# Swapping W_in's halves on VectorE instead of TensorE, in a convolution + GELU feed-forward kernel

## The chip, the cores and the metric

One core of a Trainium2 chip runs the whole kernel. The time is device microseconds of that core, the median over several executions. An execution under the hardware profiler gives the trace; all instants below are microseconds from the start of the profiled span, and an instruction's time is what the trace gives for it.

The engines: TensorE (PE) multiplies, VectorE (DVE), ScalarE (ACT) and GpSimd (POOL) work on vectors, SyncE (SP) only issues transfers. SP, ACT and POOL each have a DMA queue: q1 is SP's, q10 ACT's and q0 POOL's. All three are served by the same 16 DMA engines.

## What is computed

Input x is 8 sequences of 4096 tokens with 192 channels. A causal convolution of 7 taps runs along each sequence; its weights are a softmax over the taps, one set for each of 8 heads of 24 channels. Then a two-layer network: 192 to 2048, exact GELU, 2048 to 192.

```python
w = np.exp(weight - max) ; w = w / (sum(w) + 1e-9)        # (8 heads, 7 taps)
x_pad = zeros(6 tokens) followed by x                      # in each sequence
conv[b, s, h, g] = sum_k w[h, k] * x_pad[b, s + k, h, g]
h = conv.reshape(32768, 192) @ w_in                        # 192 x 2048
out = (gelu(h)) @ w_out                                    # 2048 x 192
```

Everything goes in and out in float32; inside, the matrices and activations that PE reads are bf16.

## The kernel before

**Layout.** The 32768 tokens are split into two halves. Partitions 0 to 63 hold channels of the first half's tokens, partitions 64 to 127 the same channels of the second half's, so that PE does two products of 64 rows side by side. 192 channels are three groups `p` of 64. The tokens go by in blocks, per half: four blocks of 256 tokens, then blocks of 512 (`WS`, L33).

**Weights in SBUF.** W_in (`win`) is loaded once, half of its columns to each half of the partitions: partitions 0 to 63 get columns 0 to 1023, partitions 64 to 127 columns 1024 to 2047 (`win_in`, L227). Each half needs the other half's columns too, so what lies on one half is copied across to the other. Before, PE does that: `dup` (L537) multiplies with an identity (`idb`), placed so that the result comes out on the opposite partitions, in PSUM, and DVE evicts it to `win` (`dup_out`, L341), in four steps of 256 columns. POOL issues the load in two parts: columns 0 to 255 of each half, then the other 768; behind them W_out (`wout`, L268).

**A block's stages.** Loads of x go into one of three buffers `xin` (`load`, L169; four DMAs for each block). DVE transposes 32x32 squares to have channels on the partitions (`trans`, L363); POOL adds the halo of six earlier tokens (`halo`, L273). The convolution of blocks 3 and on is done by DVE as 21 multiply-adds per block (`conv`, L382). That of the first three blocks (`ND`) is done by PE (`pconv`, L559): for each tap a product with a diagonal matrix (`dg`, written by `diag`, L333) of the tap's weights; the result is in PSUM and is evicted as bf16 (`conv_out`, L356; for block 0 ACT, L488). For the products, block 0's transposed x is cast by ACT (L480), that of blocks 1 and 2 by DVE (`cast`, L349).

**The network.** A block has slices: 8 of two 128-column chunks of W_in for 256 tokens, 16 of one chunk for 512. `mm1` (L599) makes a slice in one of two PSUM buffers `hp`, ACT applies GELU from PSUM into `gT` (L509), and `mm2` (L626) multiplies `gT` with W_out. The second layer of block n - 1 is spread over the slices of block n; in block 1 it starts at slice 2 and first waits for W_out. A group `g` is 128 tokens of the second layer; its result is evicted by DVE (`evac`, L409) and stored by SP. Group 1 of block 0 and the products of block 2's convolution use the same PSUM buffer (`ob[1]`), so that group waits for all three evictions of block 2 (L636); the third product of block 2 waits for the eviction of the first (L573), with which it shares a bank.

**Order.** Each engine works through a list written by hand, in order. PE: 5 spins (products whose result nobody reads), the products that spread the tap weights, 8 spins, block 0's convolution with the first swap step inside, then the slices; the table `behind` (L594) says which swap step or convolution stands behind which slice: swap steps 1 to 3 behind slices 1 to 3 of block 0, block 1's three products behind slices 4 to 6, block 2's behind slices 1 to 3 of block 1. DVE: the softmax's small operations, `diag`, block 0's transposes, the swap evictions, blocks 1 and 2, then the convolutions of block 3 and on, with the evictions `evac` at the places that the table `late` gives as (block, operation). SP: x for block 0 and, when the first part of W_in has landed, for blocks 1, 2, 3; then one further load and one store for each block (L687 on). Of blocks 0 and 1, ACT issues half of the loads.

**Tap weights.** The softmax gives 8x7 numbers on 8 partitions. Each channel's partition needs those of its head: POOL makes a 0/1 matrix `sel` with two selects (L237, L247), PE multiplies (L529), and DVE copies the result to `wcol` (L329).

Of the kernel before, what the change touches and what calls it, by code (L numbers as in the profile page):

```python
# [5 lines left out]
ALU = mybir.AluOpType  # L6
AF = mybir.ActivationFunctionType
BF16 = mybir.dt.bfloat16
F32 = mybir.dt.float32


def bass_lightweight_conv__then__act_gelu_exact_kernel(
# [76 lines left out]
    with es:  # L89
# [7 lines left out]
        wnm = sbt("wnm", [H, KS], F32)  # L97
        sel = sbt("sel", [H, NP * 128], F32)
        wcol = sbt("wcol", [128, NP * KS], F32)
# [15 lines left out]
        S_WIN = [sem("S_WIN%d" % i) for i in range(2)]  # L115
# [4 lines left out]
        S_SEL = sem("S_SEL")  # L120
        S_IDN = sem("S_IDN")
        S_PEP = sem("S_PEP")
# [5 lines left out]
        S_CAST = sem("S_CAST")  # L128
        S_PC = sem("S_PC")
        S_PCE = sem("S_PCE")  # L130
        S_DUP = sem("S_DUP")
# [13 lines left out]
        DUPB = [hp[0], ob[1], ob[0], ob[1]]  # L145
# [8 lines left out]
        FH = F // 2  # L154

# [70 lines left out]
        def _(g):  # L226
            def win_in(c0, c1, sm):  # L227
# [5 lines left out]

            win_in(0, FQ, S_WIN[0])
            g.wait_ge(S_MSET, 2)
            pat = [[64, NP], [0, 2], [1, 64]]
            g.affine_select(  # L237
                out=sel[:, :],
                in_=sel[:, :],
                compare_op=ALU.is_ge,  # L240
                fill=0.0,
                base=0,
                pattern=pat,
                channel_multiplier=-GRP,
            ).then_inc(S_SEL)
            g.wait_ge(S_SEL, 1)
            g.affine_select(  # L247
                out=sel[:, :],
                in_=sel[:, :],
                compare_op=ALU.is_ge,  # L250
                fill=0.0,
                base=GRP - 1,
                pattern=[[-a, b] for a, b in pat],
                channel_multiplier=GRP,
            ).then_inc(S_SEL)
            for hf in range(2):
# [10 lines left out]
            win_in(FQ, FH, S_WIN[1])  # L267
            g.dma_start(  # L268
                ap(wout, 0, [[NF * C, 128], [C, NF], [1, C]]),
                ap(woutt, 0, [[C, 128], [128 * C, NF], [1, C]]),  # L270
            ).then_inc(S_WOUT, 16)
# [36 lines left out]
            for n in range(NB):  # L308
                halo(n)

        @block.vector
        def _(v):
            v.memset(warm[:, :], 0.0).then_inc(S_WARM)  # L313
            v.memset(sel[:, :], 1.0).then_inc(S_MSET)
            v.memset(idb[:, :], 1.0).then_inc(S_MSET)
            v.wait_ge(S_WSB, 16)
# [7 lines left out]
            v.wait_ge(S_PRO, 3)  # L324
            v.tensor_scalar(
# [7 lines left out]
            def diag(p):  # L333
# [4 lines left out]
                    ALU.mult,  # L338
                ).then_inc(S_DG)

            def dup_out(s):  # L341

                v.wait_ge(S_DUP, s + 1)
                v.tensor_copy(  # L344
# [386 lines left out]
```

## Time and profile before

| | us |
|---|---|
| median of 11 runs (lowest to highest) | 700.83 (699.98 to 702.55) |
| the profiled execution: its time | 700.38 |
| its span, first to last instruction | 698.6 |
| first slice of block 0 starts | 12.79 |
| first slice of block 2 starts | 39.03 |
| first slice of block 4 starts | 61.76 |
| W_out: issued, landed | 5.67, 25.2 |

The page of the profile gives each engine's busy time as a share of the span and the chain of work that ended last, followed back from the end, with shares by engine. The same chain can be listed in order of time: each row gives a start, a duration, and the engine, the tile written and the line. A window's row gives, for a stretch of the span, the busy time of PE, of PE's weight loads, of DVE, ACT and POOL (with instructions in brackets), then the granted clock, the mean share of the DMA engines and GB/s. Rows of the timeline give start, duration, engine, line, operation and tiles; several like instructions are merged (x2), and what stands in brackets is the idle time of the engine before and what ended it. An instruction's duration includes some 0.1 us in which the next already starts, so a run of like instructions is costed by the distance of their starts.

### The profile page before, as it was taken

To read this page: it belongs to the slowest core of one execution; us is meant where nothing else is said; L and a number is where in the kernel's file an instruction comes from. 1 tells how busy PE (TensorE), PEld (TensorE's weight loads), DVE (VectorE), ACT (ScalarE), POOL (GpSimd) and SP (SyncE) were. 2 spreads that over 40 slices of the span, in tenths; PEclk is the share of its full clock that TensorE was granted. 3 is DMA by queue.
4 is the path that set the end of the run, shared out by engine and by line. 5 is a ranking of instruction groups with operands and counts; after the bars stand their busy time and mean duration, and the time that the engine had idled before them with its cause. 6 is when DMAs were issued, how large, how long until landed. Compare 5 with 4: busy or idle time off the path is not lost.

```text
span 698.6 us, 25401 instructions
## 1 busy us (share of the span) xinstructions
PE 689.3 (99%) x11625; PEld 529.2 (76%) x11625; DVE 551.7 (79%) x908; ACT 529.1 (76%) x524; POOL 39.7 (6%) x87
## 2 busy tenths in 40 slices
PE   8999999999999999999999999999999999999998
PEld 4797677777777777777777777777777777777777
DVE  3599978898888898888898888898888898888811
ACT  4577877777777777777777777777777777777771
POOL 4100000000000000000000000000000000000000
PEclk9999999999999999999999999999999999999999
DMA  9758433555433555434455443555533455521013
GB/s 203 156 134 194 115 76 88 123 136 137 118 87 85 122 136 137 118 76 97 120 137 137 114 97 84 117 137 136 123 92 82 115 137 136 127 58 25 23 48 92
DMA packets 22666, 78.15 MB, mean 112 GB/s; under 512 B 6944, under 2 KB 10784, under 8 KB 18720
## 3 DMA queue, kind: packets, MB, share of 16 engines
q1 hardware_dynamic: 18832, 73.80, 44.6%
q0 software_dynamic: 2896, 1.57, 1.6%
q8 instruction: 91, 1.49, 0.9%
q10 hardware_dynamic: 832, 1.16, 0.6%
q14 instruction: 15, 0.12, 0.1%
HBM read 52.92 MB, written 25.17 MB: 112 GB/s over the span
## 4 chain that ended last, share of the span: by engine, by line
PE 96%; DVE 3%; issue 1%; POOL 0%; ACT 0%; POOLq 0%; DVEq 0%
PE ob L650 48%; PE hp L616 46%; DVE acc L403 1%; PE ob L579 1%; PE hp L523 1%; DVE xT L373 0%; DVE xc L403 0%; DVE acc L396 0%; PE ob L529 0%; POOL win L229 0%; DVE osb L412 0%; ACT gT L509 0%; DVE win L344 0%; PE ob L551 0%; POOL sel L237 0%
## 5 line engine op out<-in xcount | busy, mean ns | idle before, releaser
L509 ACT ACTIVATE gT<-hp 128x1024 bf16<-128x1024 f32 x512 | 523.5, 1024 | 148.8 <-PE hp L616 148.8
L650 PEld LDWEIGHTS ob<-wout,gT 64*128 64x128 bf16 x8192 | 367.9, 94 | 100.2 <-issue 0.8
L650 PE MATMUL ob<-wout,gT 64*128 64x192 bf16 x8192 | 428.1, 243 | 0.2
L616 PE MATMUL hp<-xc,win 64*128 64x512 bf16 (+1 forms) x3264 | 423.0, 363 | 3.6 <-DVE xc L403 1.6
L403 DVE SCALAR_TENSOR_TENSOR acc<-xT,wcol,acc 128x512 f32<-128x512 f32 (+1 forms) x465 | 311.2, 734 | 0.0
L616 PEld LDWEIGHTS hp<-xc,win 64*128 64x128 bf16 x3264 | 165.4, 94 | 57.0 <-ACT gT L509 4.3
L412 DVE COPY osb<-ob 128x384 f32<-128x384 f32 x128 | 70.5, 551 | 125.3 <-PE ob L650 125.1
L403 DVE SCALAR_TENSOR_TENSOR xc<-xT,wcol,acc 128x512 bf16<-128x512 f32 (+1 forms) x93 | 63.5, 736 | 0.0
L373 DVE STREAM_TRANSPOSE xT<-xin 128x512 f32<-128x512 f32 (+1 forms) x102 | 61.2, 650 | 0.0
L396 DVE TENSOR_SCALAR acc<-xT,wcol 128x512 f32<-128x512 f32 (+1 forms) x93 | 54.1, 633 | 1.1
L302 POOL COPY xT<-xT 128x558 f32<-128x558 f32 x31 | 20.3, 654 | 590.2 <-DVE xT L373 590.2
L285 POOL COPY xT<-xT 128x18 f32<-128x18 f32 x28 | 11.2, 401 | 0.0
L579 PE MATMUL ob<-xTb,dg 64*64 64x256 bf16 x126 | 9.1, 293 | 0.3 <-DVE xTb L351 0.3
L579 PEld LDWEIGHTS ob<-xTb,dg 64*64 64x64 bf16 x126 | 6.9, 116 | 2.8 <-issue 1.1
L359 DVE CAST xc<-ob 128x256 bf16<-128x256 f32 x6 | 2.5, 422 | 6.7 <-PE ob L579 6.7
L523 PE MATMUL hp<-warm 128*128 128x512 bf16 x13 | 5.9, 630 | 1.3 <-DVE warm L313 1.3
L344 DVE CAST win<-ob 128x768 bf16<-128x768 f32 x3 | 2.9, 952 | 3.6 <-PE ob L551 3.6
L523 PEld LDWEIGHTS hp<-warm 128*128 128x128 bf16 x13 | 1.6, 139 | 3.8 <-issue 2.5
L296 POOL CAST xTb<-xT 128x186 bf16<-128x186 f32 x9 | 3.4, 386 | 14.6 <-DVE xT L373 14.6
L488 ACT ACTIVATE xc<-ob 128x256 bf16<-128x256 f32 x3 | 1.2, 384 | 3.3 <-PE ob L579 3.3
L344 DVE CAST win<-hp 128x768 bf16<-128x768 f32 x1 | 1.0, 958 | 3.3 <-PE hp L551 3.3
L480 ACT ACTIVATE xTb<-xT 128x256 bf16<-128x256 f32 x3 | 1.1, 418 | 2.9 <-DVE xT L373 2.9
(34 smaller groups left out, 21.5 us busy)
## 6 DMA issues: line engine op xcount, KB each, us to landing
xin<-in_x_dram SPq DMA_DIRECT2D x120, 380.0 KB, 6.7
out_dram<-osb SPq DMA_DIRECT2D x116, 192.0 KB, 3.1
xin<-in_x_dram SPq DMA_DIRECT2D x12, 188.0 KB, 7.4
out_dram<-osb SPq DMA_DIRECT2D x40, 48.0 KB, 1.8
wout<-in_moe_w_out_dram POOLq DMA_DIRECT2D x1, 768.0 KB, 19.5
xin<-in_x_dram ACTq DMA_DIRECT2D x4, 188.0 KB, 5.2
win<-in_moe_w_in_dram POOLq DMA_DIRECT2D x2, 288.0 KB, 6.3
out_dram<-osb ACTq DMA_DIRECT2D x8, 48.0 KB, 2.0
```

Of the source, the lines that this page charges most:

```text
L285: g.tensor_copy(dst, ap(xT[(n - 1) % 2], WS[n - 1] + 31, [[NP * XW, 128], [XW, NP], [32, HB]],),).then_inc(S_HALO)
L302: g.tensor_copy(ap(t, 1, [[NP * tw, 128], [tw, NP], [32, HB], [1, 31]]), ap(t, WS[n], [[NP * tw, 128], [tw, NP], [32, HB], [1, 31]]),).the ...
L344: v.tensor_copy(ap(win, FH + s * FQ, [[NP * F, 128], [F, NP], [1, FQ]]), ap(DUPB[s], 0, [[1024, 128], [FQ, NP], [1, FQ]]),).then_inc(S_DUPE)
L373: v.transpose(ap(xT[n % 2], p * XW + HL, [[NP * XW, 128], [1, w]]), ap(xin[n % NX], 64 * p, [[TB // 32 * D, 128], [D, w // 32], [1, 32]],) ...
L396: ins = v.tensor_scalar(a, src, wk, None, ALU.mult)
L403: ins = v.scalar_tensor_tensor(dst, src, wk, a, op0=ALU.mult, op1=ALU.add)
L412: v.tensor_copy(ap(osb[m % 2], g * C, [[8 * C, 128], [4 * C, 2], [1, C]]), ap(ob[(G0[m] + g) % 2], 0, [[1024, 128], [512, 2], [1, C]]),).t ...
L509: a.activation(out=ap(gT[n % 2], i * c * 2 * w, dst), in_=ap(hp[u % 2], 0, src), func=AF.Gelu,).then_inc(S_GELU)
L523: t.matmul(hp[1][:, 0:512], warm[:, 0:128], warm[:, :])
L579: ins = t.matmul(b[r, o : o + w], dg[r, d0 : d0 + 64], xTb[n][r, x0 : x0 + w], start=(k == KS - 1), stop=(k == 0), tile_position=(64 * hf, ...
L616: ins = t.matmul(hp[u % 2][:, hf * TB + cc * w : hf * TB + cc * w + w], win[r, p * F + wcols(hf, f0) : p * F + wcols(hf, f0) + 128], xc[n ...
L650: ins = t.matmul(ob[gg % 2][:, 512 * sub : 512 * sub + C], gT[m % 2][r, c0 : c0 + 128], wout[r, CH[i] * C : (CH[i] + 1) * C], start=(ph == ...
```

## The change

The swap of W_in moves from PE to DVE. The matmuls `dup` and the PSUM evictions `dup_out` go. Instead DVE copies, for each part of W_in, the 64 partitions of one half straight to the other half within SBUF, bf16 to bf16: two copies for each of three parts (columns 0 to 255, 256 to 511, 512 to 1023 of each half). The load of W_in comes in the same three parts, one semaphore each.

The tap weights are spread by DVE: `wnm` is now a 32x32 tile of zeros with the softmax in its corner; it is transposed, each head's column is copied 24 times along the free axis, and four transposes of 32 partitions put the weights on the channels' partitions. `sel`, its two selects, the products and the copy from PSUM go; `wcol` has 32 columns per group instead of 7.

PE runs 16 spins in one row. `pconv` now does one tap at a time and waits for the halo only at the second tap; the 21 taps of block 1 are spread over slices 2 to 6 of block 0, those of block 2 over slices 1 to 4 of block 1. Slices 0, 2 and 4 of block 0 wait for the parts of W_in and for their copies.

On DVE, block 1's work stands behind two of the three swaps; block 2's evictions `conv_out` move into block 3's operations, before operations 2, 5 and 8 (three transposes, then the convolution's taps). Block 0's groups are evicted at operations 9 and 16 of block 3 instead of 4 and 14.

The queues: POOL issues all of W_in, then block 0's halo, then W_out. SP issues its half of block 1's load without a wait, block 2's load when the last part of W_in has landed, and block 3's when W_out has landed; the loads and stores after that follow it.

```diff
-        wnm = sbt("wnm", [H, KS], F32)
-        sel = sbt("sel", [H, NP * 128], F32)
-        wcol = sbt("wcol", [128, NP * KS], F32)
+        wnm = sbt("wnm", [32, 32], F32)
+        wnt = sbt("wnt", [32, 32], F32)
+        wch = sbt("wch", [32, D], F32)
+        wcol = sbt("wcol", [128, NP * 32], F32)
...
+        FP = [0, FQ, 2 * FQ, FH]
...
-            win_in(0, FQ, S_WIN[0])
-            g.wait_ge(S_MSET, 2)
...
+            win_in(FP[0], FP[1], S_WIN[0])
+            g.wait_ge(S_MSET, 1)
...
-            win_in(FQ, FH, S_WIN[1])
-            g.dma_start(
-                ap(wout, 0, [[NF * C, 128], [C, NF], [1, C]]),
-                ap(woutt, 0, [[C, 128], [128 * C, NF], [1, C]]),
-            ).then_inc(S_WOUT, 16)
+            win_in(FP[1], FP[2], S_WIN[1])
+            win_in(FP[2], FP[3], S_WIN[2])
...
-            for n in range(NB):
+            halo(0)
+            g.dma_start(
+                ap(wout, 0, [[NF * C, 128], [C, NF], [1, C]]),
+                ap(woutt, 0, [[C, 128], [128 * C, NF], [1, C]]),
+            ).then_inc(S_WOUT, 16)
+            for n in range(1, NB):
                 halo(n)
...
-            v.wait_ge(S_PEP, 1)
-            v.tensor_copy(wcol[:, :], ob[0][:, 0 : NP * KS]).then_inc(S_PRO)
+            v.transpose(wnt[:, :], wnm[:, :]).then_inc(S_PRO)
...
+            v.tensor_copy(
+                ap(wch, 0, [[D, 32], [GRP, H], [1, GRP]]),
+                ap(wnt, 0, [[32, 32], [1, H], [0, GRP]]),
+            ).then_inc(S_PRO)
...
+            for q in range(4):
+                v.transpose(
+                    ap(wcol, 32 * q * NP * 32, [[NP * 32, 32], [1, NP * 32]]),
+                    ap(wch, 32 * (q % 2), [[D, 32], [64, NP], [1, 32]]),
+                ).then_inc(S_PRO)
...
-            def dup_out(s):
-
-                v.wait_ge(S_DUP, s + 1)
-                v.tensor_copy(
-                    ap(win, FH + s * FQ, [[NP * F, 128], [F, NP], [1, FQ]]),
-                    ap(DUPB[s], 0, [[1024, 128], [FQ, NP], [1, FQ]]),
-                ).then_inc(S_DUPE)
+            def dup(s):
+
+                v.wait_ge(S_WIN[s], 32)
+                for hf in range(2):
+                    v.tensor_copy(
+                        ap(
+                            win,
+                            64 * (1 - hf) * NP * F + FH + FP[s],
+                            [[NP * F, 64], [F, NP], [1, FP[s + 1] - FP[s]]],
+                        ),
+                        ap(
+                            win,
+                            64 * hf * NP * F + FP[s],
+                            [[NP * F, 64], [F, NP], [1, FP[s + 1] - FP[s]]],
+                        ),
+                    ).then_inc(S_DUPE)
...
-            for q in range(3):
-                dup_out(q)
-            for n in range(1, ND):
-                for p in range(NP):
-                    trans(n, p)
-                for p in range(NP):
-                    cast(n, p)
-                if n == 1:
-                    dup_out(3)
-                for p in range(NP):
-                    conv_out(n, p)
-
-
-            late = {(0, 0): (3, 4), (0, 1): (3, 14), (1, 0): (4, 1), (1, 1): (4, 9)}
+            dup(0)
+            dup(1)
+            for p in range(NP):
+                trans(1, p)
+            for p in range(NP):
+                cast(1, p)
+            dup(2)
+            for p in range(NP):
+                conv_out(1, p)
+            for p in range(NP):
+                trans(2, p)
+            for p in range(NP):
+                cast(2, p)
+
+
+            late = {(0, 0): (3, 9), (0, 1): (3, 16), (1, 0): (4, 1), (1, 1): (4, 9)}
...
+                    if b == ND and o in (2, 5, 8):
+                        conv_out(ND - 1, o // 3)
...
-            spin(5)
-            t.wait_ge(S_SEL, 2)
-            t.wait_ge(S_PRO, 4)
...
-            spin(8)
...
+            for i in range(16):
+                t.matmul(hp[1][:, 0:512], warm[:, 0:128], warm[:, :])
...
+                if k == KS - 1:
+                    t.wait_ge(S_CAST[n], p + 1)
+                    if n == 0:
+                        t.wait_ge(S_DG, p + 1)
+                    elif n == 2 and p == 0:
+                        t.wait_ge(S_PCE, 2 * NP)
+                    elif n == 2 and p == 2:
+                        t.wait_ge(S_PCE, 2 * NP + 1)
+                if k == KS - 2:
+                    t.wait_ge(S_HALO, HC[n] + 2 + p)
...
+            taps = [(p, k) for p in range(NP) for k in range(KS - 1, -1, -1)]
+            for p, k in taps:
+                pconv(0, p, k)
+
+            behind = {}
+            for n, i0, i1 in ((1, 2, 7), (2, 1, 5)):
+                for i in range(i0, i1):
+                    j0 = len(taps) * (i - i0) // (i1 - i0)
+                    j1 = len(taps) * (i + 1 - i0) // (i1 - i0)
+                    behind[n - 1, i] = [(n, *q) for q in taps[j0:j1]]
...
-                if n == 0 and i % 2 == 0:
-                    t.wait_ge(S_DUPE, i // 2 + 1)
+                if n == 0 and i in (0, 2, 4):
+                    t.wait_ge(S_WIN[i // 2], 32)
+                    t.wait_ge(S_DUPE, 2 * (i // 2) + 2)
...
             load(sp, 0, (0, 1))
-            sp.wait_ge(S_WIN[0], 32)
             load(sp, 1, (0, 1))
+            sp.wait_ge(S_WIN[2], 32)
             load(sp, 2)
+            sp.wait_ge(S_WOUT, 16)
             load(sp, 3)
```

## The prediction

> **What bounds the kernel now.** I read the page's busy shares and chain first, then the chain in order of time, then windows over the first 100 us, last the DMA queues.
>
> ```profile
> PE 689.3 (99%) x11625; PEld 529.2 (76%) x11625; DVE 551.7 (79%) x908; ACT 529.1 (76%) x524; POOL 39.7 (6%) x87
> ...
> PE 96%; DVE 3%; issue 1%; POOL 0%; ACT 0%; POOLq 0%; DVEq 0%
> ```
>
> TensorE (PE) is the chain for 96% of the span. The change leaves the matmuls of the steady blocks alone, so the time moves by what it does to the start. My marker is block 2's first slice, at 39.03 in the chain in order of time (start us, us, what):
>
> ```profile
> 8.95 2.26 PE ob L579 x22
> ...
> 11.47 0.86 PE ob L579 x15
> ...
> 14.76 0.97 DVE win L344
> ...
> 18.06 1.09 DVE xT L373 x3
> ...
> 24.47 1.03 ACT gT L509
> ...
> 39.03 0.66 PE hp L616 x12
> ```
>
> Before the marker the chain leaves PE for the eviction of swapped W_in, for block 1's transposes queued behind it, and for a gelu. The first row also shows the conv taps at 103 ns each and the later one at 57. The granted clock reads 1.00 in every window, but by these durations the array ran at half rate until about 10.9, some 5.5 us after unbroken matmuls began at 5.36 (the spins before were cut by 1.8 us of tiny float32 matmuls).
>
> Windows tell whether time won before 39.03 survives:
>
> ```profile
> 24.30:39.03 14.73, 14.16 (x274) 11.77 (x272) 8.98 (x24) 8.95 (x9) 2.10 (x6) 1.00 0.38 87
> 39.03:49.55 10.52, 10.52 (x229) 9.95 (x226) 10.32 (x21) 7.95 (x9) 1.01 (x2) 1.00 0.74 174
> 49.55:60.40 10.85, 10.70 (x225) 10.18 (x220) 10.62 (x18) 8.24 (x9) 0.00 (x0) 1.00 0.75 176
> 60.40:61.80 1.40, 0.04 (x2) 0.07 (x4) 1.40 (x3) 0.36 (x1) 0.00 (x0) 1.00 0.57 135
> ```
>
> PE is full but for 1.4 us at 60.4, where block 4 waits for VectorE's (DVE's) convolution. DVE is busy without a gap from the second eviction of block 0 (39.07, which waits for PE) to there. So both engines hang on PE's state at the marker: a marker G earlier ends the kernel G earlier, the 1.4 us kept.
>
> **The change, part by part.**
>
> *Weights.* Gone: six float32 matmuls, two POOL selects (0.6 each), the 0.38 memset and the PSUM copy that ended at 5.64. Added after `wnm` (3.41): a 32x32 transpose, a 192-element copy, four 96-element transposes. None is in the trace; below stands the one-column row (0.15), above the 256-element transpose (0.33 start to start). I take 0.2, 0.28 and 4 x 0.24, with waits 1.5: 4.95, 0.7 earlier (ends: 4.4 to 5.6). Then diag 0 and 1 (0.54 each) end at 6.15 and the first transpose waits for block 0's input, which lands near 6.45 (issue at 1.7, 4.8 to landing). It gains 0.3, no more.
>
> *Warm-up.* Sixteen unbroken spins from 1.26 at 0.427 end at 8.1 if all run slow; full rate after 5.5 us, as before, is 6.8, and the spins then end at 7.45. The casts of block 0 are ready then (before: waiting from 7.7 until 8.88 for PE). 42 taps at 57 ns are 2.4: PE is through at 9.9, ScalarE's last eviction (0.39) at 10.3. Before it was 12.74.
>
> *The swap of W_in.* Out: 24 matmuls and four evictions from PSUM of 0.96. In: six DVE copies of 64 partitions, four of 768 and two of 1536 elements. No SBUF-to-SBUF copy of bf16 is in the trace. Nearest are these, float32 from SBUF:
>
> ```profile
> 32.88 0.83 DVE L396 TENSOR_SCALAR acc<-xT,wcol 128x256 f32<-128x256 f32 x1
> 32.90 0.66 POOL L302 COPY xT<-xT 128x558 f32<-128x558 f32 x1 [7.13 <-DVE xT L373]
> ...
> 34.70 0.61 DVE L396 TENSOR_SCALAR acc<-xT,wcol 128x256 f32<-128x256 f32 x2
> ```
>
> Undisturbed, 256 elements take 0.27 start to start against 0.42 for the cast from PSUM: two elements per cycle. That makes 768 elements 0.5 and 1536 0.9. [...] The PSUM row would make them 0.96 and 1.75. [...] I take 0.37 and 0.57; by the two-per-cycle row the last swap ends 0.7 later, slice 4 some 0.3 late. [...]
>
> When do they start? The first piece of W_in landed at 9.3 (issue 2.1, 7.2). Half of block 1's load (two DMAs of 188 KB) no longer waits for it and now runs ahead: at the 0.225 MB/us of 4 to 8 us, 0 to 1.7 later; I take 0.6, so 9.9. First swap done at 10.7, block 0's first slice at **10.8** (before 12.79). The second piece lands near 11, swapped by 11.75; block 1's transposes and casts (1.05 and 0.9) to 13.75; the third piece: 2.31 MB now lie ahead of and in it, and before 2.27 MB moved from 2.0 to 12.4, so it lands about 13.3; its swap runs 13.75 to 14.9.
>
> *Blocks 0 and 1 on PE.* Two slices 1.48; slice 2 waits for the first gelu (12.7). Slices 2 to 6 carry 0.76 and four taps of 0.125, 1.26 each; slice 4 at 15.25 is past the last swap. Slice 7 ends at 19.9, block 1's first slice starts there (before 24.35). Its second waits for gelu to 21.05; taps follow slices 1 to 4, five, five, five and six. The fifteenth is due at 25.8. From it to the marker: 0.125 + six taps 0.75, slices 4 to 7 2.7, second-layer matmuls (54 pairs at 0.083) 4.6: 8.2. Marker 34.0, **5.0 earlier**, if nothing else waits.
>
> *The wait that appears.* That fifteenth tap needs PSUM freed by block 2's first eviction, which the new order puts behind two of block 3's transposes on DVE (1.15 from the load's landing to the tap). These need block 3's load, which SP now issues only when W_out has landed; W_out itself is issued by POOL behind block 0's halo (about 8.4 instead of 5.67) and lies behind W_in. Queued behind SP's wait are block 4's load, needed at 39 and landing near 32, and the stores, not due before 30. So W_out must land by 18.75 for block 3's 752 KB, which take 5.9 (a quiet queue at 41.4 us: 4.1 for the first 380 KB, 6 for 760), to come by 24.65.
>
> Before, W_out landed at 25.2, but against three x loads. Who had the DMA engines from 8 to 12 us, and then from 13 to 21 (packets, MB, share)?
>
> ```profile
> q0 software_dynamic: 1028, 0.80, 128.0%
> q10 hardware_dynamic: 2, 0.00, 0.1%
> ```
>
> ```profile
> q1 hardware_dynamic: 440, 1.79, 93.4%
> q0 software_dynamic: 490, 0.19, 18.9%
> ```
>
> SP had issued x loads from 9.31 on, yet W_in and W_out (q0) kept the engines alone for 3.5 us; only then did packets go one for one, x's of 6 KB against W_out's of 384 bytes. After the change SP issues block 2's load when W_in's last piece lands, 13.3. With the same delay its packets begin at 16.8, and W_out, alone from 12.4 at 0.19 MB/us (0.37 MB in the 1.9 us before 12.8), has moved its 0.79 MB by 16.6. Its last increment came 2.3 after its packets thinned out at 22.9; so it lands at **18.9**. Block 3's load lands at 24.8, the tap runs at 25.95 instead of 25.8: 0.2 late. The other consumer (the second group's matmuls, which want all three of block 2's evictions, 4.66 after the load) is due at 30.1 and met at 29.5. Block 2's own load lands near 20.6, its first cast at 21.9, just when its first tap is due.
>
> **Sum.** 5.0 - 0.2 = 4.8: marker 34.2. Hidden at no cost: the finer tap order, the third W_in piece (two more issues of 0.65 on POOL, over before the transposes reach it), the later evictions of block 0; uncovered, each is under 1.3. The profiled execution took 700.38 (span 698.6); 700.38 - 4.8 = 695.6. The median of the runs is 0.45 above it: **696.0**.
>
> **Rivals.** *W_out is starved* (24%): block 2's packets begin soon after their issue (1.1 us in a quiet queue at 41.4) and W_out trickles as from 13 to 21. Both together, 1.56 MB from 12.4 at 0.2475 MB/us, end at 18.7; with 0.5 for the hand-over and 1.0 to landing 20.2, block 3 at 26.1, the tap at 27.3: 1.5 of 5.0 lost, 697.3. For it the second of the two queue answers, against it the first. *Swaps at one element per cycle* (12%): as in the PSUM row; across partitions nothing in the trace excludes it. First slice 11.85, last swap 15.7 to 19.2, slice 4 at 19.25 instead of 15.25: 4.0 of 5.0 is lost, and block 3's load is then hidden: 699.8, no change that can be seen. *The serial loads cost more than the start gains* (9%): from a W_out landing at 23.9 on, block 3 comes after 29.8 and the marker is no earlier. At 25.2, where it landed before, the tap waits until 32.3 and the marker is 40.5, 1.5 late: 702.3, slower. For it: that landing; against it, only one x load now competes. *That the change does nothing*: excluded for the start, since the evictions on the chain are gone.
>
> **Chances and range.** The forecast 55%, the others as said. 0.2% (1.4 us) is about what a measurement tells from none. The forecast's own span is 694.8 to 697.2: marker 33 (first slice at 10.2, nothing late) to 35.4. Faster: 55 + 24 = 79%, same 12%, slower 9%. The range 694.6 to 699.9 takes in the third case's middle and leaves out the slow one and the tails.
>
> **What would show it.** Taps at 57 ns before 9; first slice at 10.8; swaps of 0.37 and 0.57; W_out landing near 19, block 3's last packet near 24.5; PE nearly without idle in block 1; marker at 34.2; the 1.4 before block 4 kept. It is wrong if W_out lands later by over 1.5 us, if the copies go at PSUM pace, or if DVE's gap-free stretch starts later than PE allows.

## The result, and the profile after

The changed kernel takes 698.78 us (median of 13 runs, 697.66 to 699.61) against 701.09 for the kernel before beside it: a ratio of 0.9958, 95% interval 0.9946 to 0.997. It is faster by 0.3% to 0.5%, a gain of 2.3, a little under half of the 4.8 that was forecast. In the profiled execution the span went from 698.6 to 696.8 and the time from 700.38 to 698.73. The marker, block 2's first slice, starts at 36.34 instead of 39.03; the forecast was 34.2.

The page after, busy times and the shares of the chain:

```profile
PE 686.9 (99%) x11598; PEld 528.2 (76%) x11598; DVE 552.3 (79%) x915; ACT 528.5 (76%) x524; POOL 39.9 (6%) x87
...
PE 94%; DVE 2%; DMA 2%; issue 1%; POOL 1%; SPq 0%; POOLq 0%; DVEq 0%
```

TensorE (PE) is still the chain for nearly all of the span; its busy time fell by 2.4. The chain in order of time (start, duration, what) has other links than before, though: loads, and two long rows of "issue" (30.29 and 48.91), in which PE waited for nothing that the profile shows.

```profile
5.17 7.74 DMA win<-in_moe_w_in_dram
...
14.21 7.24 DMA xin<-in_x_dram
21.47 1.10 DVE xT L375 x3
22.57 0.24 DVE xTb L353
...
30.29 0.37 issue
...
36.34 0.65 PE hp L588 x12
...
48.91 0.81 issue
...
58.87 0.74 DVE xc L405
```

Windows of the changed kernel: block 1's second slice to the marker, block 2, block 3, the wait ahead of block 4. The last three are the stretches that the prediction showed for the kernel before; its first window began one slice earlier, at block 1's first.

```profile
21.91:36.34 14.43, 13.83 (x258) 11.25 (x260) 9.57 (x26) 7.87 (x8) 2.28 (x6) 1.00 0.52 121
36.34:46.87 10.53, 10.53 (x228) 9.96 (x226) 9.54 (x19) 7.95 (x9) 1.00 (x2) 1.00 0.72 165
46.87:58.36 11.49, 10.68 (x224) 10.17 (x220) 10.60 (x17) 8.18 (x9) 0.00 (x0) 1.00 0.82 187
58.36:59.78 1.42, 0.02 (x2) 0.05 (x4) 1.39 (x3) 0.40 (x1) 0.00 (x0) 1.00 0.23 66
```

The kernel before, from block 1's second slice to the marker:

```profile
25.54:39.03 13.49, 13.35 (x258) 11.24 (x260) 7.74 (x20) 7.88 (x8) 1.11 (x4) 1.00 0.31 71
```

The changed kernel needs 14.43 where that one needs 13.49, for the same 258 recorded matmuls. The wait of 1.4 ahead of block 4 is still there. Block 3 takes 11.49 where it took 10.85, and PE's idle time in it is the row at 48.91. So the lead on the kernel before (starts of the slices' first weight load) rises and then shrinks:

| slice starts at | before | after | lead |
|---|---|---|---|
| block 0, first | 12.78 | 11.30 | 1.5 |
| block 1, first | 24.25 | 20.62 | 3.6 |
| block 1, second | 25.54 | 21.91 | 3.6 |
| block 2, first | 38.79 | 36.09 | 2.7 |
| block 4, first | 61.73 | 59.73 | 2.0 |
| block 6, first | 98.58 | 96.58 | 2.0 |

From block 4 to the last slices the lead stays 2.0; of it 1.8 is left in the span and 1.65 in the profiled time. Three things need a cause: where 2.8 of the 4.8 went, whether the parts of the change are worth anything alone, and whether W_out is as safe as in this execution.

### The profile page after: what moved, and what is told of

It reads as the page before. It is cut to its first block, busy times and chain, and to the rows that moved or that the text cites. A ratio compares the mean times of both kernels' runs of the same rounds, so it can differ in the third digit from the quotient of the medians.

```text
span 696.8 us, 25348 instructions
## 1 busy us (share of the span) xinstructions
PE 686.9 (99%) x11598; PEld 528.2 (76%) x11598; DVE 552.3 (79%) x915; ACT 528.5 (76%) x524; POOL 39.9 (6%) x87
## 4 chain that ended last, share of the span: by engine, by line
PE 94%; DVE 2%; DMA 2%; issue 1%; POOL 1%; SPq 0%; POOLq 0%; DVEq 0%
PE ob L622 48%; PE hp L588 45%; DVE acc L405 1%; DMA win<-in_moe_w_in_dram 1%; DMA xin<-in_x_dram 1%; POOL win L227 0%; DVE xT L375 0%; PE ob L548 0%; DVE xc L405 0%; DVE acc L398 0%; SPq L173 0%; DVE osb L414 0%; POOL idb L236 0%; DVE xTb L353 0%; POOLq L236 0%
## 5 line engine op out<-in xcount | busy, mean ns | idle before, releaser
L515 ACT ACTIVATE gT<-hp 128x1024 bf16<-128x1024 f32 x512 | 523.0, 1023 | 149.4 <-PE hp L588 149.4
L277 POOL COPY xT<-xT 128x558 f32<-128x558 f32 x31 | 20.2, 652 | 586.9 <-DVE xT L375 586.9
L338 DVE COPY win<-win 64x768 bf16<-64x768 bf16 (+1 forms) x6 | 3.1, 509 | 2.3 <-DMA win<-in_moe_w_in_dram 2.1
L227 POOL DMA_DIRECT2D win<-in_moe_w_in_dram x6 | 3.9, 655 | 0.8 <-POOLq L689 0.8
```

The costliest lines, as they stand in the source:

```text
L227: g.dma_start(ap(win, 64 * hf * NP * F + c0, [[NP * F, 64], [F, NP], [1, c1 - c0]]), ap(wint, hf * FH + c0, [[F, 64], [64 * F, NP], [1, c1 ...
L277: g.tensor_copy(ap(t, 1, [[NP * tw, 128], [tw, NP], [32, HB], [1, 31]]), ap(t, WS[n], [[NP * tw, 128], [tw, NP], [32, HB], [1, 31]]),).the ...
L515: a.activation(out=ap(gT[n % 2], i * c * 2 * w, dst), in_=ap(hp[u % 2], 0, src), func=AF.Gelu,).then_inc(S_GELU)
```

## The experiments

**The parts alone.** Three kernels put one part of the change each into the kernel before.

The swap by VectorE (DVE) alone, with the old weights and queues (the cut shows the copies; PE's products `dup` and their semaphore go with it):

```diff
-                v.wait_ge(S_DUP, s + 1)
-                v.tensor_copy(
-                    ap(win, FH + s * FQ, [[NP * F, 128], [F, NP], [1, FQ]]),
-                    ap(DUPB[s], 0, [[1024, 128], [FQ, NP], [1, FQ]]),
-                ).then_inc(S_DUPE)
+                v.wait_ge(S_WIN[min(s, 1)], 32)
+                for hf in range(2):
+                    v.tensor_copy(
+                        ap(win, 64 * (1 - hf) * NP * F + FH + s * FQ, [[NP * F, 64], [F, NP], [1, FQ]]),
+                        ap(win, 64 * hf * NP * F + s * FQ, [[NP * F, 64], [F, NP], [1, FQ]]),
+                    ).then_inc(S_DUPE)
```

> The kernel before, with only the swap moved to VectorE (four steps of two copies, at the old places in its list); tap weights, warm-up, loads and the order behind the slices as before. My theory (the swap's PSUM evictions cost the start some 2 us, since block 1's transposes stood behind them): block 0's third slice starts at 14.3 instead of 15.8 (it then waits for the first gelu only), block 1's first slice near 22.3 instead of 24.3, and the kernel is about 2.0 us faster than before. Rival (the gain of the change comes from the loads and the warm-up, the swap is hidden): block 1's first slice stays within 0.5 of 24.3 and the time within 0.7 us of before.

Measured: 705.93 (4 runs) against 700.79, ratio 1.0071 (1.0056 to 1.0086): slower. Block 1's first slice did start 2.3 earlier, at 21.91, but then PE stood still for 4.70 from 26.57. The chain in order of time of this kernel:

```profile
5.65 25.57 DMA wout<-in_moe_w_out_dram
31.27 1.78 PE ob L623 x20
```

One row covers 25.57: W_out, issued at 5.65, landed at 31.22 (before: 25.21). The DMA queues of this kernel between 17 and 26 us (packets, MB, share):

```profile
q1 hardware_dynamic: 352, 1.96, 93.1%
q0 software_dynamic: 615, 0.24, 21.4%
```

While x's packets were pending, W_out (q0, packets of 384 bytes) moved 0.24 MB in 9 us. What had changed is x: DVE had taken block 1's x from its buffer earlier, so block 4's load was issued at 16.84 instead of 19.17. The kernel before had moved as little of W_out in that stretch (0.25 MB); the difference lies in its end. From 23 to 27 us x and W_out went packet for packet here (119 against 115), and there only 13 of W_out's packets were left. So before, W_out's last packets got through ahead of block 4's; here the two ended together (31.22 and 31.04).

The weights by DVE and the unbroken spins alone, with the old swap and queues:

```diff
-            spin(5)
-            t.wait_ge(S_SEL, 2)
-            t.wait_ge(S_PRO, 4)
...
-            spin(8)
+            for i in range(16):
+                t.matmul(hp[1][:, 0:512], warm[:, 0:128], warm[:, :])
```

(and the transposes, copies and memsets of the diff that stand for `sel` and its products)

> The kernel before, with only the tap weights spread by VectorE and the sixteen unbroken spins; the swap stays on TensorE. My theory: the array is at full rate before block 0's convolution, whose taps then take 57 ns and not 103; the first swap step waits for W_in at 9.3, so block 0's first slice starts near 11.3 instead of 12.8, and the whole is 1.0 to 1.4 us faster. Rival (block 1's input, which lands at 15.8, and the swap's evictions set the pace anyway): the first slice moves, block 1's first slice moves by under 0.5 and the time is within 0.5 us of before.

Measured: 704.37 (4 runs), ratio 1.0051 (1.0036 to 1.0066): slower too, by the same mechanism. Block 4's load was issued at 17.50, W_out landed at 30.93, PE paused 3.75. After that pause the clock counts as well. Windows of this kernel, the last but two columns being the granted clock:

```profile
17.00:40.00 23.00, 18.44 (x285) 14.00 (x282) 9.44 (x26) 9.95 (x11) 3.25 (x10) 0.85 0.58 124
40.00:60.00 20.00, 19.93 (x426) 18.67 (x422) 19.25 (x39) 14.79 (x15) 1.00 (x2) 1.00 0.57 135
```

The clock lacks 0.15 of 23 us, which is 6.9 us at half clock. Some 1.7 of them lie in the pause itself (granted clock 0.78 from 27.23 to 30.98), the others slow the matmuls behind it (0.50 from 30.98 to 36).

The queues' new order alone:

```diff
-            g.dma_start(
-                ap(wout, 0, [[NF * C, 128], [C, NF], [1, C]]),
-                ap(woutt, 0, [[C, 128], [128 * C, NF], [1, C]]),
-            ).then_inc(S_WOUT, 16)
...
-            for n in range(NB):
+            halo(0)
+            g.dma_start(
+                ap(wout, 0, [[NF * C, 128], [C, NF], [1, C]]),
+                ap(woutt, 0, [[C, 128], [128 * C, NF], [1, C]]),
+            ).then_inc(S_WOUT, 16)
+            for n in range(1, NB):
...
-            sp.wait_ge(S_WIN[0], 32)
             load(sp, 1, (0, 1))
+            sp.wait_ge(S_WIN[1], 32)
             load(sp, 2)
+            sp.wait_ge(S_WOUT, 16)
             load(sp, 3)
```

> The kernel before with the new order of queues alone: W_out issued behind block 0's halo; block 1's first half load no longer behind W_in's first piece; block 3's load behind W_in's second piece and W_out. Swap by TensorE and the old weights stay. Theory (the queues only protect, the gain is the swap's and the weights' work): W_out lands by 19, no pause before the second layer, block 1's first slice still starts at 24.0 to 24.9, since the swap's evictions and block 1's transposes on VectorE set it; the time is that of the kernel before, 0 to 0.8 us less. Rival (the queues are themselves the gain): 1.5 us or more faster than before. Rival (W_in's first piece, disturbed by block 1's half load, sets the start): block 1's first slice 0.6 or more later and the time 0.5 or more us slower than before.

Measured: 700.6 (10 runs), ratio 0.9991 (0.9979 to 1.0004): no difference. W_out landed at 18.13, seven us earlier than before, and block 1's first slice started at 24.45, as the theory had it. Alone, the queues' order buys nothing.

**The rest without the queues.** The changed kernel with POOL's and SyncE's (SP's) old order; W_in still in three parts:

```diff
+            g.dma_start(
+                ap(wout, 0, [[NF * C, 128], [C, NF], [1, C]]),
+                ap(woutt, 0, [[C, 128], [128 * C, NF], [1, C]]),
+            ).then_inc(S_WOUT, 16)
...
-            halo(0)
-            g.dma_start(
-                ap(wout, 0, [[NF * C, 128], [C, NF], [1, C]]),
-                ap(woutt, 0, [[C, 128], [128 * C, NF], [1, C]]),
-            ).then_inc(S_WOUT, 16)
-            for n in range(1, NB):
+            for n in range(NB):
...
+            sp.wait_ge(S_WIN[0], 32)
             load(sp, 1, (0, 1))
-            sp.wait_ge(S_WIN[2], 32)
             load(sp, 2)
-            sp.wait_ge(S_WOUT, 16)
             load(sp, 3)
```

> The changed kernel with only its queues put back: POOL issues W_out ahead of block 0's halo, SP waits for W_in's first piece before block 1's load and then for nothing else before blocks 2 and 3. Theory from the two kernels with one part of the change alone: what lets the gain through is that W_out no longer shares the DMA engines with three x loads. Here it does: it lands past 28, TensorE stands 4 to 6 us in block 1 before the second layer, and the kernel is 2 to 6 us slower than before. Rival (the two parts alone were slow for reasons of their own, the load order is worth little): block 1 without such a wait and a time within 1.5 us of the changed kernel's.

Measured: 703.99 (10 runs), ratio 1.0041 (1.0027 to 1.0055). W_out landed at 31.23, block 1's first loads at 15.49; PE paused 2.07 at 29.21 for W_out, less than was expected, and 3.15 at 13.74 for block 1's x, which was not expected. The parts do not add:

| time, us | old queues | new queues |
|---|---|---|
| old swap and weights | 700.8 | 700.6 |
| new swap and weights | 704.0 | 698.8, and 699.6 in the second set below |

The faster start is worth 1.0 to 1.8 with the new order and costs 3.2 with the old. Two things change with the order, W_out's place and when SP issues its half of block 1's load; the table does not part them.

**One wait put back.** The changed kernel, where SP again waits for W_in's first part ahead of its half of block 1's load:

```diff
             load(sp, 0, (0, 1))
+            sp.wait_ge(S_WIN[0], 32)
             load(sp, 1, (0, 1))
```

> The changed kernel with SP waiting for W_in's first piece before its half of block 1's load, as in the kernel before. Theory: W_in's first piece lands 0.5 to 1.0 earlier (9.3 to 9.8 instead of 10.3) and block 0's first slice 0.4 earlier, but block 1's load comes behind W_in and W_out's packets, past 15; its casts stand ahead of the last swap in VectorE's list, so block 0's fifth slice waits to 17 or later instead of 15.9, and the time is 0.5 to 2.5 us above the changed kernel's. Rival (the early load only takes bandwidth from W_in): a gain of 0.3 to 0.8 us.

Measured: 703.67 (10 runs), ratio 1.0038 (1.0022 to 1.0054). W_in's parts landed at 9.15, 9.73 and 11.57, earlier by 1.1 to 1.3, and the first slice started at 10.63; the forecast's delay of W_in by that load is real and was guessed too small (0.6). But block 1's x, issued from 9.17 on, moved no packet before 12 us, while W_in and W_out had the DMA engines. It landed at 16.81, and PE paused 4.80 at 13.42. The early load costs 0.7 at the first slice and saves the pause. The kernel is 4.1 to 4.9 slower than the changed one, where 0.5 to 2.5 was expected, although W_out is in its new place. So the early load is a condition of the gain, and its lack explains the longer pause of the kernel with the old queues. W_out in its old place with the early load was not run; what that place alone costs is not shown.

**The changed kernel again**, without an edit.

> The changed kernel once more, unaltered. Instruction fetch theory: its pauses stand at the same places in TensorE's list, the boundaries of 256 instructions (the fifth slice of block 1 and the third of block 3), and only their length differs, 0.2 to 0.6 and 0.5 to 1.0, with when the x load before them ends. Rival (disturbances from outside): pauses at other places or none. W_out lands between 17 and 21.5; where it is past 20, TensorE waits in block 1 for block 2's first eviction. Time 0.3 to 0.5% below before.

Measured: 699.57 (10 runs, 698.42 to 702.26), ratio 0.9972 (0.9953 to 0.9991). In its profile W_out landed at 20.43 where the first profile has 17.07. Its chain in order of time:

```profile
8.91 11.52 DMA wout<-in_moe_w_out_dram
...
21.73 4.82 DMA xin<-in_x_dram
26.56 0.77 DVE xT L375 x2
27.33 0.32 DVE xc L361
```

Of the 16 increments of W_out's semaphore 14 had come by 17.7; the last two came near 20.4, behind packets of block 2's x. SP issued block 3's load only then; it landed at 26.54 and PE stood for 0.91 before the fifteenth tap of block 2. This is the wait that the prediction built for that tap; W_out landed a little later than even the starved rival had it (20.2), and the wait lies between the forecast's 0.2 and that rival's 1.5. The pauses of "issue" were not as expected: none near 30, and 0.17 at 49.20. The two executions lost the time in different places, and their spans are 696.8 and 696.5.

**The wait for W_out taken away.** The changed kernel without it:

```diff
-            sp.wait_ge(S_WOUT, 16)
             load(sp, 3)
```

> The changed kernel without SyncE's wait for W_out ahead of block 3's load. Theory (the wait makes block 3's load as late as W_out's last straggler, 17 in one run and 20.4 to 21.3 in two others): block 3's load lands at 24.0 to 24.6 whatever W_out does, W_out's last packets land by 24, before the second layer wants them at about 25; no pause before the fifteenth tap; 0.3 to 1.0 us below the changed kernel, 1.0 in the runs in which that one has the pause. Rival (the wait protects W_out): block 3's packets take W_out's turns, W_out lands after 25, TensorE pauses 1 us or more before the second layer of block 0, and the time is 1 to 5 us above the changed kernel's.

Measured: 698.31 (10 runs, 697.55 to 699.2), ratio 0.9953 (0.9939 to 0.9967). W_out had stragglers at 21.61 and 24.50, block 3's load landed at 24.96, and there was no wait before the tap or before the second layer. (Pauses of "issue" there were, 0.59 at 30.18 and 0.81 at 49.02.) Both landings are later than the theory said, with little to spare, but they are in time. The median is 0.5 and 1.3 below the two sets of the changed kernel and the runs lie closer together; the intervals overlap, so the gain is likely and not shown.

**The pauses of "issue".** PE's rows at 30.29 and 48.91 lie 765 recorded instructions apart; the kernel before has a small one (0.11 at 50.21) at the place of the second. A queue of its own, marked "instruction", moves packets of 16 KB, 91 of them in the execution. PE's 23196 recorded matmuls and weight loads are 255 for each packet, and 765 is three times that (the recorded expectations say 256). So a packet is taken here to be a fetch of PE's next 255 or so instructions, and a boundary to be the place in PE's list where such a block ends. That is an estimate from the size, the counts and the times; no view names what a packet holds. PE crossed one boundary near 36.6, and a packet began at 36.88. For the pause at 48.91, the DMA queues of the changed kernel from 43 to 47 us, and then from 47 to 48.4:

```profile
q1 hardware_dynamic: 109, 0.94, 106.0%
```

```profile
q1 hardware_dynamic: 306, 0.20, 62.7%
q8 instruction: 1, 0.02, 6.1%
```

PE crossed the boundary before this one near 42.7. No instruction packet moved while block 5's x filled the engines (0.94 MB from 43 to 47); it started at 47.04, when that load had ended, took 1.4 to 48.40, and PE went on at 49.71.

The packets' times fit in the other executions too. The profiles of ten, the kernel before included, show twelve such pauses in the first 60 us, and in each PE goes on 2.5 to 2.9 after its packet has begun: here at 30.66 and 49.71, after packets that began at 27.9 and 47.0; in the kernel before at 50.32, after 47.6. In the second execution of the changed kernel the packet for the first of these boundaries moved at 23.0, in a gap that the late W_out had left between two loads, and there was no pause. The other one began at 46.8, and the pause was 0.17.

The next kernel moves block 5's load behind the first store that follows it:

```diff
+                if n == 2:
+                    store_group(sp, 1, 0)
+                    load(sp, 5)
+                    store_group(sp, 1, 1)
+                    continue
```

> The changed kernel, with block 5's load of x moved behind the first store of block 1 on SP's queue (some 4 us later). It tests what the pause of 0.80 us in block 3 (third slice, at 48.9) is. Instruction fetch theory: TensorE's next 256 instructions are asked for at 42.7 and their packet gets through only when block 5's load has ended (47.0); with the load later the packet starts within 1 us of 42.7, the pause is under 0.15, block 4 starts about 0.8 earlier than in the changed kernel and the time falls by 0.5 to 0.9 us. Rival (the pause is a wait for a semaphore or a buffer of the order itself): it stays at the same slice with 0.7 to 0.9 us.

Measured: 698.97 (10 runs), ratio 0.9966 (0.9947 to 0.9986): no better than the changed kernel. The pause at that boundary was gone: the packet moved at 45.21, just after it was due. But the load, issued from 47.63 on with block 6's behind it from 51.92, now covered the next boundary, and the chain has this row in its place:

```profile
57.31 1.53 issue
```

The pause follows the loads. In this execution W_out also came late, at 21.31, and PE waited 1.55 for block 3, the same mechanism as above; so the time does not tell what the load's place is worth.

**The wait ahead of block 4.** DVE reaches block 4 late because it stands in evictions of the second layer until PE has finished them. The timeline of DVE in the changed kernel, what stands in brackets being the idle time before the row:

```profile
53.13 0.56 DVE L414 COPY osb<-ob 128x384 f32<-128x384 f32 x1 [0.86 <-PE ob L622]
53.61 3.39 DVE L405 SCALAR_TENSOR_TENSOR acc<-xT,wcol,acc 128x512 f32<-128x512 f32 x5
```

Four such waits (0.73, 1.52, 0.92, 0.86) add up to 4.0. The next kernel has the evictions later in DVE's list:

```diff
-            late = {(0, 0): (3, 9), (0, 1): (3, 16), (1, 0): (4, 1), (1, 1): (4, 9)}
-            late.update({(2, 0): (4, 16), (2, 1): (4, 23), (3, 0): (5, 14), (3, 1): (6, 1)})
+            late = {(0, 0): (3, 11), (0, 1): (3, 21), (1, 0): (4, 6), (1, 1): (4, 13)}
+            late.update({(2, 0): (4, 20), (2, 1): (5, 1), (3, 0): (5, 15), (3, 1): (6, 2)})
```

> The changed kernel, with the evictions of the second layer of blocks 0 to 3 two to six operations later in VectorE's list, and block 2's second one in block 5. My theory: the 1.40 us that TensorE waits before block 4 is VectorE's, and VectorE lost 4.0 us from 31 to 53 waiting for TensorE in evictions that came up too early; without these waits its convolution of block 4 is done before TensorE needs it: the 1.40 falls under 0.2, and the time is 1.2 to 1.7 us under the changed kernel's. Rival (VectorE's work alone is too long for blocks 4 and 5): the wait stays above 1.0 and the time within 0.4 us of the changed kernel's.

Measured: 696.72 (4 runs), ratio 0.9948 (0.9933 to 0.9963). The 1.40 ahead of block 4 is gone (block 4's first slice at 57.29); ahead of block 5 there is a wait of 0.49 instead of 0.17. Block 6 starts at 94.51, 2.1 earlier than in the changed kernel. Not all of that is the evictions' doing: the pauses of "issue" were 0.52 in this execution and 1.18 in that of the changed kernel. The intervals of the two kernels' times overlap; that the wait goes is shown by the trace.

**Put together.** First with those evictions, block 5's load in two halves around a store, and even halves in the swap's copies (below):

```diff
-                            [[NP * F, 64], [F, NP], [1, FP[s + 1] - FP[s]]],
+                            [[NP * F, 64], [(FP[s + 1] - FP[s]) // 2, 2], [F, NP], [1, (FP[s + 1] - FP[s]) // 2]],
...
+                if n == 2:
+                    load(sp, 5, (0, 2))
+                    store_group(sp, 1, 0)
+                    load(sp, 5, (1, 3))
+                    store_group(sp, 1, 1)
+                    continue
```

> The changed kernel with the later evictions, with block 5's load in two halves (the second behind the first store of block 1), and with each swap copy cut into two halves of columns, so that its outermost count is 2 and not 3. [...] Time 0.3 to 0.9 us under the kernel with the later evictions alone, 4.3 to 5.0 under before. [...]

Measured: 697.29 (7 runs, 695.33 to 699.45), ratio 0.9949 (0.9926 to 0.9972). No pause in block 3, no wait ahead of block 4, but a pause of 0.44 at 29.99, at a boundary again. The time is no better than with the later evictions alone (696.72), where 0.3 to 0.9 less was expected.

Then with block 4's load split as well and without the wait for W_out:

```diff
-            sp.wait_ge(S_WOUT, 16)
...
+                if n == 1:
+                    load(sp, 4, (0, 2))
+                    sp.wait_ge(S_TR, NP * 4)
+                    load(sp, 4, (1, 3))
+                    store(sp, 0)
+                    continue
```

> The fastest variant so far (block 0 and 1's late evictions, loads of block 5 in two halves, even halves of the swapped columns) with two more edits: block 4's load also in two halves, the second issued behind block 4's earlier transposes' release, so that an instruction packet finds a gap between them; and no wait for W_out ahead of block 3's load. If both pauses that are left near 30 are instruction fetches behind an x load, the pause of 0.44 us at 30 goes and the time is 0.3 to 0.8 us below that variant (696.5 to 697.0). If taking the wait for W_out away starves it, W_out lands after 25 and the time is 1 to 5 us above it.

Measured: 695.48 (5 runs, 695.1 to 696.01) against 700.79, ratio 0.9917 (0.9898 to 0.9937): 1.8 below the variant before it, more than was expected, and 5.3 below the kernel before. The gain on the kernel before is shown; the intervals of the two variants still touch. What of the 1.8 belongs to which of the two edits was not taken apart; the runs of the variant before spread over four us, these over one. The queues of this kernel from 41.7 to 44 us, a boundary being crossed at 41.79, and its windows over the first and third of the stretches shown above:

```profile
q8 instruction: 1, 0.02, 3.6%
```

```profile
21.75:35.46 13.71, 13.57 (x258) 11.07 (x260) 10.99 (x30) 7.88 (x8) 2.11 (x6) 1.00 0.54 127
...
46.00:56.26 10.26, 10.26 (x223) 9.70 (x221) 9.04 (x15) 7.93 (x9) 0.00 (x0) 1.00 0.96 228
```

The packet moved at 42.47, and the boundary at 47.79 was crossed without a stop. PE has no idle time at all in block 3, and the stretch up to the marker takes 13.71 where the changed kernel takes 14.43. W_out landed at 18.67 in this execution, so its profile does not try the case of late stragglers.

## Why the prediction came out as it did

The sign was right, and the forecast's direction for nearly every step, but the gain was less than half of what it said: 2.0 at block 4 and 2.3 between the medians, where the forecast said 4.8. The measured 698.8 lies in the stated range, 694.6 to 699.9, but above the forecast's own span (694.8 to 697.2). The range reached that far for the slow swaps, which did not occur, and what took the time instead was in none of the four cases. That the time fell into the range is luck. Two terms failed: the sum for PE's blocks 0 and 1, 0.9 too short, and PE's idle time in blocks 1 and 3, put at nothing, where the pauses put down to instruction packets cost 1.3 in the profiled execution. Step by step:

**Weights and warm-up: right in what they are worth.** The four transposes are 0.30 apart instead of 0.24, so `diag` starts at 5.36 instead of 4.95. It does not matter, because block 0's input landed at 6.51 (forecast 6.45). PE's timeline:

```profile
1.26 6.54 PE L528 MATMUL hp<-warm 128*128 128x512 bf16 x16 [1.26 <-DVE warm L293]
7.74 2.48 PE L548 MATMUL ob<-xTb,dg 64*64 64x256 bf16 x42
11.33 1.49 PE L588 MATMUL hp<-xc,win 64*128 64x256 bf16 x24 [1.12 <-DVE win L338]
```

The taps run at 59 ns from 7.74, full rate, as the step said (57). The last spin ended 0.35 late.

**The swap: the copies' rate and the landing were off by half a microsecond.** DVE's timeline:

```profile
10.31 1.77 DVE L338 COPY win<-win 64x768 bf16<-64x768 bf16 x4 [2.13 <-DMA win<-in_moe_w_in_dram]
...
14.08 1.40 DVE L338 COPY win<-win 64x1536 bf16<-64x1536 bf16 x2
```

Copies of 768 elements are 0.45 apart (0.42 each), those of 1536 are 0.72 apart (0.685 each), where the forecast had taken 0.37 and 0.57. The 0.37 and 0.57 were the author's estimate: no row of the kernel before gives them, and no copy of the changed kernel ran at that pace. 768 elements more take 0.27 more, 0.35 ns each. In the kernel before a cast from PSUM takes 0.42 for 256 and 0.96 for 768, 1.05 ns each, the pace that the prediction calls one element per cycle. Its float32 row from SBUF takes 0.345 for 256 and 0.475 for 512 where POOL copies nothing beside it, 0.51 ns each, the pace that the prediction calls two. The estimate amounts to 0.20 for 768, 0.26 ns each; the copies came out between it and the float32 row. The shape matters: the copy has three rows (`NP`), and the kernels with the same columns as two even halves took 0.355 and 0.554, 0.20 for 768 more, and their shorter copies stand 0.39 apart, close to the forecast's estimate of 0.37. Why three rows are slower than two halves is not shown. The first part of W_in landed at 10.29 instead of 9.9, which is the larger part of the loss. Together the first slice came at 11.30 instead of 10.8: **0.5 lost**. "Swaps at one element per cycle" is excluded.

**Blocks 0 and 1 on PE: the sum of pieces was too short.** Slices 2 to 6 of block 0 are 1.315 apart instead of 1.26, and block 1's second slice starts 10.61 after the first slice of block 0 instead of 10.25: 0.36 lost. From there to the marker the sum gave 13.15; the same stretch, with 258 matmuls recorded in each trace, took 13.49 before (25.54 to 39.03) and 13.71 in the last variant, which has no pause there: 0.56 lost. The failing steps are "1.26 each", "the fifteenth is due at 25.8" and "8.2". The stretch was put together from some twenty small terms. The second layer's share, "54 pairs at 0.083" (which is 4.5, not 4.6), leaves out that two of its runs of 22 matmuls stop for the half of the layer ahead of them (`S_PH`): they take 1.25 and 1.15, the others 0.91. That is 0.58 together, and the chain of before has both. The difference of two starts in that chain would have given 13.49 at once. **0.9 lost** in all.

**"PE nearly without idle in block 1" and "a marker G earlier ends the kernel G earlier" failed**, and this is the largest term. Block 2's load landed at 21.45 instead of 20.6, so its first tap waited 0.11. The pause at 30.29 took 0.37 and the 22 matmuls around it took 1.56, pause included, where others took 0.91: about 0.6. The one at 48.91 took 0.81, against 0.11 before, so 0.7 of the lead went after the marker. **1.4 lost** in this execution; in the second one these pauses cost little and W_out's tail, 0.91, took their place. The loads' new places relative to PE's list did it: a kernel that moves its loads also moves which of the list's boundaries they cover. The forecast asked only what the transfers do to data. That the pause is a fetch behind a load rests on its place, on the packets' times in ten executions and on three kernels in which moving or splitting the load moved or removed it.

These sum to 0.5 + 0.9 + 1.4 = 2.8, and 4.8 - 2.8 = 2.0, the lead at block 4.

**The wait that appears: right in place, and its size varies.** Who has the DMA engines in the changed kernel from 13 to 17 us:

```profile
q0 software_dynamic: 1607, 0.61, 127.6%
q1 hardware_dynamic: 70, 0.32, 24.4%
```

W_out ran nearly alone, as the first of the prediction's two queue answers has it, and landed at 17.07 (forecast 18.9); block 3's load landed at 24.49 (24.8), in time for the tap. But x's first packets came at 15.5 to 16.2, not at 16.8, when some hundred packets of W_out were still to go. In two other executions with the same start a few of these went one for one with x's and landed at 20.4 and 21.3. So the rival "W_out is starved" is no other mechanism but the tail of the forecast's own; it costs PE a wait of 0.91 or 1.55 when it comes, and after the 1.55 a slower clock too (below). "The serial loads cost more than the start gains" did not occur. What the rivals missed is that the queues' order, block 1's early load included, is no risk beside the gain but the condition for it: without it the same start makes the kernel 3.2 slower.

**"The 1.4 before block 4 kept": right**, and it could be had: DVE's wait comes from PE's second layer through the evictions, and later evictions took it away.

## What to carry to other kernels

Where a start is made faster, work out what its earlier releases let loose: here the two kernels with one part of the change and the old queues emptied x's buffers sooner and lost more to a late W_out than the start had gained, and with both parts and the old queues block 1's x came too late as well. Price a stretch by one window's row over the same work in the trace of before, and the edit by its difference from it, rather than by a sum of small rows. Look in the chain for rows of "issue" at equal distances in an engine's list, and keep big loads from covering those places, in halves if need be.

## What the runs showed of the hardware that was not expected

Instruction packets came late behind loads that filled the DMA engines: PE stopped for up to 1.53 at boundaries, some 255 recorded instructions apart, when a block's load (1.5 MB for 512 tokens) covered the time in which the packet was due, and not at all at 47.79 in the last variant, whose packet had found a gap at 42.47. From the packet's start until PE went on it was 2.5 to 2.9 in all twelve pauses.

The copy of three rows of bf16 takes 0.420 for 768 elements, the same elements as two halves 0.355.

Behind some pauses of PE the clock was lower too. Worked out from the granted clock of windows around them, the array was at half rate for 6.8 to 6.9 with pauses of 3.75 to 4.80 (the first 0.9 to 1.7 of that still in the pause), and for about 3.5 behind pauses of 1.55 and of 3.15. It stayed at a granted clock of 1.00 behind pauses of 0.91 and 1.40, but also behind one of 1.53 and one of 2.07. So the length of the pause alone does not decide it; what does is not shown. At the start, the distance of the spins falls from 0.427 to 0.216 at anything from 3.3 to 5.9 after the first of the same 16 spins, in ten executions, so a forecast to a few tenths was not to be had there.
